# Tanh over runs of up to six W1 items, and the last output block's products and stores, in a fused attention and MLP kernel

## The chip, the cores and the metric

One core of one Trainium2 chip. The metric is the device time of one execution in microseconds (us). The engines are TensorE (PE, matrix products into the eight PSUM banks), VectorE (DVE), ScalarE (ACT), GpSimd (POOL) and SyncE (SP, which issues the transfers between HBM and the on-chip memory SBUF). Each engine works through its own instruction stream in order and waits on semaphores for the others.

## The reference

`x` is [1, 2048, 1024] in bf16, F is 3584, there are 32 heads of 32. The kernel computes

```
xn = layernorm(x)
s  = attention(xn; wqkv) @ wo            # softmax over 2048 keys, 32 heads
h  = gelu(layernorm(xn) @ w1 + b1)       # tanh form of gelu
g  = silu(h @ w2 + b2)
out = x + s * g
```

`layernorm` subtracts the mean and divides by the square root of variance + 1e-5, `gelu` is the approximation 0.5 x (1 + tanh(0.798 (x + 0.0447 x^3))).

## The kernel before, in words

**Two streams of work.** Attention runs over 8 groups of 4 heads, 8 blocks of 256 queries and 8 pairs of key blocks, 512 units in all. For each unit TensorE forms the scores of four heads (L902), ScalarE takes the exponential in two instructions over 128x1024 (L911), TensorE multiplies with V (L625), and VectorE adds the probabilities in a tree (L928, L942) from which TensorE forms the row sums. The last block of 256 queries is done in two halves of 128 (`half_unit`, L1197, with its scores at L1211 and exponentials at L1221), each closed by `half_quotient` (L1241): two 32x32 transposes, a reciprocal and a product on VectorE. Six PSUM banks hold scores, banks 6 and 7 take everything else in turn ("dense" work): projections, the MLP, P·V, the output projection.

**The MLP** runs beside attention in 8 chunks of 256 rows. A chunk has 14 W1 items (`w1_item`, L1074): sixteen matmuls of 128x128 by 256 columns into one bank (L630), then VectorE adds the bias and writes one of 20 slots of `hT` (L1084). Item p of the whole run uses slot p mod 20. Gelu follows on runs of neighbouring slots: five VectorE operations (L1098 square, L1099 times constant plus 1, L1100 times x, L1102 plus 1, L1103 times x) around one tanh on ScalarE (L1101) in one of two buffers `ut` of four items each. A run ends at every fourth slot, at a chunk's end, and at some fixed places, so it has four items (2048 elements a partition) or two (1024). The four W2 items of a chunk (`w2_item`, L1106) then read all its 14 slots, 56 matmuls each, and silu follows with one tanh per two items (L1128). `seq_mlp` (L1140) gives the order: six W1 items of the next chunk stand between the first three W2 items of this one and its fourth, eight behind that.

**What sets the order.** A planner written in Python (`_Plan`) simulates the five engines when the kernel is built, with a cost for every instruction, and emits each engine's stream as it comes out, with semaphore waits from declared reads and writes (tokens). ScalarE takes exponentials first (priority 0); a tanh that has been ready for 2500 ns of planned time goes ahead of them (L160). On TensorE scores go first, then P·V and dense items by position. So a change of one instruction can move all that follow. SP, too, gets one stream: weights, stores and loads stand in it in planned order, and a store that waits holds up those behind it.

**The end.** Output rows come in 16 blocks of 128; a block has two halves of 512 columns. Each half is eight products (one for each head group, `hc` 0 to 7) with the `wo` rows. For the last four blocks (`late`) the first seven go early into a bank as an item `most`, whose sum VectorE takes out to an f32 buffer `xf`, times 0.5 and the gate (L1439), and adds x (L1442). The eighth waits for the last attention quotient and goes alone into another bank; VectorE multiplies it by 0.5 and the gate (L1452) and adds `xf` (L1455). For the very last half (row block 15, second half, `i2 == 3`) ScalarE takes the eighth product out instead (L1447), and VectorE multiplies by the gate (L1449). The last two blocks, 14 and 15, are stored in four half stores `osl0` to `osl3` (L1458), each of 128x512. Each of them is declared to write the token list `rt` of its block's buffer, which the two halves of a block share; the second half's store therefore waits for the semaphore of the first half's.

Of the kernel before, what the change touches and what calls it, by code (L numbers as in the profile page):

```python
# [7 lines left out]
ALU = mybir.AluOpType  # L8
# [459 lines left out]
def bass_recurrent_scan__mha_block__mixer_channel_mlp__prompt_kernel(  # L468
# [31 lines left out]
    with ExitStack() as st:  # L500
# [60 lines left out]
        iota_i = ut_t[0][:].rearrange("p a b -> p (a b)")[:, 0:256].bitcast(I32)  # L561

        def bank(i, lo=0, hi=512):
            return ps[:, i * 512 + lo:i * 512 + hi]
# [498 lines left out]
        def make_y(c):  # L1063
            for t2 in range(2):
# [6 lines left out]
                dma(f"yt{t2}", lambda e, t2=t2: e.dma_start_transpose(yT[:, :, t2 * 128:(t2 + 1) * 128], yst_t[t2][:]),  # L1071
                    262144, [("yst", t2)], [("yT", t2)], occ=1300, rate=300.0, lat=2300)

        def w1_item(c, pi):  # L1074
            p = c * NW1 + pi
            gi, hs = p % NW1R, p % NH
            it = _Item("mlp")
            for f2 in range(2):
                for dc in range(DC):
                    def fn(e, b, f2=f2, dc=dc):  # L1080
                        return mm(e, bank(b, f2 * 256, (f2 + 1) * 256), w1r[:, gi, dc, f2 * 128:f2 * 128 + 128], yT[:, dc, :],
                                  dc == 0 and f2 == 0, dc == DC - 1)
# [7 lines left out]
            k = 2 if (pi == NW1 - 1 and p % 4 != 3) or (pi == 1 and c % 2) or half else 4  # L1090
            h0, n = hs - k + 1, k * 512
            hs_ = [("h", h0 + i) for i in range(k)]
            ui = geg["n"] % 2
            geg["n"] += 1
            x_ = hT[:, h0:h0 + k].rearrange("p s k t -> p (s k t)")
            u_ = ut_t[ui][:].rearrange("p a b -> p (a b)")[:, 0:n]
            gp, ga = (1.4, -1) if c == NCH - 1 and pi >= 5 else (3, 1)
            dve(lambda e: e.tensor_tensor(u_, x_, x_, op=ALU.mult), c_b16(n), hs_, [("ut", ui)], gp)  # L1098
            dve(lambda e: e.tensor_scalar(u_, u_, GA, 1.0, op0=ALU.mult, op1=ALU.add), c_b4(n), [("ut", ui)], [("ut", ui)], gp)  # L1099
            dve(lambda e: e.tensor_tensor(u_, u_, x_, op=ALU.mult), c_b16(n), [("ut", ui)] + hs_, [("ut", ui)], gp)  # L1100
            act(lambda e: e.activation(u_, u_, ACT.Tanh, scale=GC), c_acts(n), [("ut", ui)], [("ut", ui)], ga)  # L1101
            dve(lambda e: e.tensor_scalar_add(u_, u_, 1.0), c_b4(n), [("ut", ui)], [("ut", ui)], gp)  # L1102
            dve(lambda e: e.tensor_tensor(x_, u_, x_, op=ALU.mult), c_b16(n), [("ut", ui)] + hs_, hs_, gp)  # L1103
            return it

        def w2_item(c, q):  # L1106
# [211 lines left out]
        for w in range(HG):  # L1318
# [24 lines left out]
            for qb in range(NQB):  # L1343
# [44 lines left out]
                for t2 in range(2):  # L1388
# [16 lines left out]
                    for nh in range(2):  # L1405
                        late = qb >= NQB - 2
                        fin = qb == NQB - 1
                        it = _Item("wo", 64 * 7 + 8 * qb + 4 * t2 + 2 * nh)
                        i2 = 2 * t2 + nh
                        sl_ = slice(nh * 512, (nh + 1) * 512)  # L1410
                        if late:
                            most = _Item("wo", it.pos + 64)
                            plan.dense["last"].append(most)
                            if fin:
                                it.bank = 2 + 2 * t2 + nh
                                if not t2:
                                    it.due = 64 * HG - 2
                            (plan.dense["wo"] if not fin else lates if t2 else firsts).append(it)
                        for hc in range(HG):
                            def fn(e, b, hc=hc, tb=tb, nh=nh, late=late):  # L1420
# [3 lines left out]
                            chunk(most if late and hc < HG - 1 else it, fn, Q512,  # L1424
                                  [("OTr", hc) if hc < 7 else ("OTr", 7, qb) + ((t2,) if fin else ()), ("wo", hc)],
                                  [("S", 1 + t2, nh)] if fin and hc == HG - 1 else ())
                        if not late:
                            dve(lambda e, it=it, gr=gr, sl_=sl_: e.scalar_tensor_tensor(gr[:, sl_], bank(it.bank), 0.5,
                                                                                        gr[:, sl_], op0=ALU.mult, op1=ALU.mult),
                                c_ps(512), [], [("gr", ri, nh)], 0, it)  # L1430
                            dve(lambda e, xr=xr, gr=gr, sl_=sl_: e.tensor_tensor(xr[:, sl_], gr[:, sl_], xr[:, sl_], op=ALU.add),
                                c_b16(512), [("gr", ri, nh)], [("xr", ri, nh)], 1)
# [6 lines left out]
                        dve(lambda e, most=most, gr=gr, sl_=sl_, xf=xf: e.scalar_tensor_tensor(  # L1439
                            xf, bank(most.bank), 0.5, gr[:, sl_], op0=ALU.mult, op1=ALU.mult),  # L1440
                            c_ps(512), [("gr", ri, nh)], [("xf", xk)] + (zs if fin else []), 0, most)
                        dve(lambda e, xr=xr, sl_=sl_, xf=xf: e.tensor_tensor(xf, xf, xr[:, sl_], op=ALU.add),  # L1442
                            c_f32(512), [("xr", ri, nh)], [("xf", xk)], 2)
                        if fin and i2 == 3:
                            hs_ = fl3(PR[0])[:, i2 * 512:(i2 + 1) * 512]
                            after([("half", i2)], [("PR", 0)])
                            act(lambda e, it=it, hs_=hs_: e.activation(hs_, bank(it.bank), ACT.Copy, scale=0.5), c_act(512),  # L1447
                                [], [("half", i2)], 1, it)
                            dve(lambda e, gr=gr, sl_=sl_, hs_=hs_: e.tensor_tensor(gr[:, sl_], gr[:, sl_], hs_, op=ALU.mult),  # L1449
                                c_b16(512), [("half", i2)], [("gr", ri, nh)], -1 + 0.1 * i2)  # L1450
                        else:
                            dve(lambda e, it=it, gr=gr, sl_=sl_: e.scalar_tensor_tensor(gr[:, sl_], bank(it.bank), 0.5,  # L1452
                                                                                        gr[:, sl_], op0=ALU.mult, op1=ALU.mult),
                                c_ps(512), [], [("gr", ri, nh)], -1 if fin and t2 else 0, it)
                        dve(lambda e, xr=xr, gr=gr, sl_=sl_, xf=xf: e.tensor_tensor(xr[:, sl_], gr[:, sl_], xf, op=ALU.add),  # L1455
                            c_f32(512), [("gr", ri, nh), ("xf", xk)], [("xr", ri, nh)], -1 + 0.1 * i2 if fin and t2 else 2.05 if fin else 1)
                        if fin:
                          dma(f"osl{i2}", lambda e, xr=xr, tb=tb, sl_=sl_: e.dma_start(  # L1458
                            out2[tb * 128:(tb + 1) * 128, sl_], xr[:, sl_]), 131072, [("xr", ri, nh)], rt, prio=0, rate=390.0, lat=1000.0)
# [70 lines left out]
```

## Time and profile before

| | us |
|---|---|
| median of the runs shown | 1033.36 |
| lowest and highest of three | 1032.63, 1033.86 |
| the profiled execution | 1032.24 |
| its span, first to last instruction | 1030.3 |
| busy: TensorE, VectorE, ScalarE | 1004.7, 956.3, 1016.9 |
| mean granted TensorE clock | 0.997 |

The profile is one execution. Its page gives the busy time of each engine, the chain of work that ended last (followed back from the last instruction to what released each step), the costliest groups of instructions by line, and the transfers. A group's row reads: line, engine, operation, output tile <- input tiles, shapes, count | busy us, mean ns of one | idle us of the engine just before them, and what ended most of it. A tile's buffer number is left out. "PEld" is TensorE's weight load, which overlaps its products. Tanh instructions are the rows with `ut` (gelu) and `gw` (silu) on ScalarE.

### The profile page before, as it was taken

The numbers are of one execution on the slowest core, as the hardware profiler recorded it, in microseconds if no ns is written. First come the engines' busy times: TensorE is split into PE (matmuls) and PEld (weight loads), VectorE is DVE, ScalarE is ACT, GpSimd is POOL, SyncE is SP. The second block draws the span as 40 slices with busy tenths as digits, with TensorE's granted clock in tenths as the row PEclk, the third lists the DMA queues.
The fourth block names the chain that finished last, engine by engine and source line by source line (L and its number), as shares of the span: only waits on it lengthen the run. The fifth ranks groups of instructions, "written<-read, shape, count | busy, mean of one in ns | idle before, by whom it ended". The sixth has DMA issues, their size and how long they took to land.

```text
span 1030.3 us, 31971 instructions
## 1 busy us (share of the span) xinstructions
PE 1004.7 (98%) x14355; PEld 636.6 (62%) x14355; DVE 956.3 (93%) x1347; ACT 1016.9 (99%) x1093; POOL 11.8 (1%) x21
## 2 busy tenths in 40 slices
PE   8999999999999999999999999999999999999996
PEld 6666656666666567566665676666666665654443
DVE  8899999899899999997899989998999889978987
ACT  8999999999999999999999999999999999999996
POOL 2200000000000000000000000000000000000000
PEclk9999999999999999999999999999999999999999
DMA  8867746645765658456547576565455752974321
GB/s 222 158 156 206 200 136 182 170 117 142 204 175 154 182 157 228 125 144 188 139 126 195 143 215 173 158 177 152 118 154 167 216 168 78 279 224 124 112 91 58
DMA packets 317144, 167.75 MB, mean 163 GB/s; under 512 B 55632, under 2 KB 304976, under 8 KB 317008
## 3 DMA queue, kind: packets, MB, share of 16 engines
q1 hardware_dynamic: 317008, 165.71, 58.8%
q8 instruction: 112, 1.84, 0.7%
q14 instruction: 24, 0.20, 0.1%
HBM read 146.55 MB, written 12.06 MB: 154 GB/s over the span
## 4 chain that ended last, share of the span: by engine, by line
ACT 84%; PE 7%; DVE 5%; DMA 2%; issue 0%; SPq 0%; POOL 0%; DVEq 0%
ACT P L911 78%; PE ps L630 4%; ACT ut L1101 4%; PE ps L625 2%; ACT gw L1128 1%; PE ps L902 1%; ACT P L1221 1%; DVE PA L928 1%; DMA wv<-in_A_wqkv_dram 1%; DVE stats L837 1%; DVE PR L942 1%; DVE hT L1084 1%; DMA yst<-in_A_x_dram 1%; DVE gw L796 0%; DMA hT<-in_A_x_dram 0%; DMA xnT<-gw 0%
## 5 line engine op out<-in xcount | busy, mean ns | idle before, releaser
L911 ACT ACTIVATE P<-ps 128x1024 bf16<-128x1024 f32 x988 | 922.4, 1231 | 0.6 <-PE ps L902 0.5
L928 DVE TENSOR_TENSOR PA<-P 128x2048 bf16<-128x2048 bf16 x173 | 209.8, 1215 | 30.0 <-ACT P L911 29.5
L630 PE MATMUL ps<-yT,w1r 128*128 128x256 bf16 x1792 | 228.0, 273 | 0.9 <-DVE V L716 0.4
L630 PE MATMUL ps<-w2r,hT 128*128 128x256 bf16 x1792 | 224.3, 273 | 0.7 <-DVE nt L997 0.3
L942 DVE TENSOR_TENSOR PR<-PR,PA 128x2048 bf16<-128x2048 bf16 x173 | 209.1, 1210 | 1.2
L902 PE MATMUL ps<-QKT 32*128 32x256 bf16 x4032 | 200.4, 273 | 9.2 <-ACT P L911 7.0
L630 PEld LDWEIGHTS ps<-yT,w1r 128*128 128x128 bf16 x1792 | 164.5, 98 | 53.5 <-issue 28.1
L630 PEld LDWEIGHTS ps<-w2r,hT 128*128 128x128 bf16 x1792 | 163.0, 98 | 51.5 <-issue 31.3
L902 PEld LDWEIGHTS ps<-QKT 32*128 32x128 bf16 x4032 | 59.8, 92 | 137.3 <-ACT P L911 129.4
L625 PE MATMUL ps<-P,V 128*32 128x256 bf16 (+1 forms) x4080 | 137.2, 272 | 0.2
L630 PE MATMUL ps<-xnT,wqk 128*128 128x512 bf16 (+2 forms) x584 | 131.3, 354 | 1.1 <-DVE nv L1010 0.3
L625 PEld LDWEIGHTS ps<-P,V 128*32 128x32 bf16 x4080 | 95.6, 96 | 32.7 <-issue 22.6
L630 PE MATMUL ps<-wv,xnT 128*128 128x256 bf16 (+2 forms) x704 | 89.7, 267 | 1.6 <-DMA xnT<-gw 0.6
L630 PEld LDWEIGHTS ps<-xnT,wqk 128*128 128x128 bf16 x584 | 50.0, 98 | 50.7 <-issue 14.4
L1084 DVE TENSOR_TENSOR hT<-ps,b1T 128x512 bf16<-128x512 f32 x112 | 76.6, 684 | 3.7 <-PE ps L630 3.2
L928 DVE TENSOR_TENSOR PR<-P 128x2048 bf16<-128x2048 bf16 x60 | 72.7, 1212 | 0.1
L630 PEld LDWEIGHTS ps<-wv,xnT 128*128 128x128 bf16 x704 | 56.5, 99 | 25.6 <-issue 11.6
L1101 ACT ACTIVATE ut<-ut 128x2048 bf16<-128x2048 bf16 (+1 forms) x33 | 61.4, 1861 | 0.0
L728 DVE CAST QKT<-ps 128x512 bf16<-128x512 f32 x58 | 39.6, 683 | 1.6 <-PE ps L630 1.2
L997 DVE STREAM_TRANSPOSE nt<-ps 128x256 f32<-128x256 f32 x63 | 27.9, 442 | 13.8 <-PE ps L625 13.4
L1103 DVE TENSOR_TENSOR hT<-ut,hT 128x2048 bf16<-128x2048 bf16 (+1 forms) x33 | 34.6, 1049 | 0.1
L1098 DVE TENSOR_TENSOR ut<-hT 128x2048 bf16<-128x2048 bf16 (+1 forms) x33 | 34.7, 1050 | 0.1
(115 smaller groups left out, 584.9 us busy)
## 6 DMA issues: line engine op xcount, KB each, us to landing
w1r<-in_B_w_dram SPq DMA_DIRECT2D x112, 512.0 KB, 4.7
w2r<-in_B_w_dram SPq DMA_DIRECT2D x128, 448.0 KB, 4.5
yst<-in_A_x_dram SPq DMA_DIRECT2D x18, 256.0 KB, 4.7
wqk<-in_A_wqkv_dram SPq DMA_DIRECT2D x16, 256.0 KB, 3.7
g_scratch<-gw SPq DMA_DIRECT2D x32, 128.0 KB, 2.9
hT<-in_A_x_dram SPq DMA_DIRECT2D x14, 256.0 KB, 3.9
o_scratch<-ot SPq DMA_DIRECT2D x56, 64.0 KB, 3.6
xnT<-o_scratch SPq DMA_DIRECT2D x7, 512.0 KB, 5.3
```

The costliest lines, as they stand in the source:

```text
L625: ins = e.matmul(dst(j), lhsT=lhsT(j), rhs=rhs(j), start=start, stop=stop, tile_position=(0, 32 * j), skip_group_check=True)
L630: return e.matmul(dst, lhsT=lhsT, rhs=rhs, start=start, stop=stop, skip_group_check=True)
L728: dve(lambda e: e.tensor_copy(QKT[sl][:, which, tq * 512:(tq + 1) * 512], bank(it.bank)), c_ps(512), [], [(nm, sl, 2 * tq), (nm, sl, 2 * t ...
L902: ins = e.matmul(bank(b0[j], kk * 256, (kk + 1) * 256), lhsT=QKT[sl][32 * j:32 * j + 32, 1, kb * 128:(kb + 1) * 128], rhs=QKT[sl][32 * j:3 ...
L911: x = act(lambda e, h=h: e.activation(Pt[pi][:, 2 * h:2 * h + 2].rearrange("p j k q -> p (j k q)"), ps[:, pr[h] * 1024:(pr[h] + 1) * 1024] ...
L928: return dve(lambda e: e.tensor_tensor(dst[:].rearrange("p u j q -> p (u j) q"), src[:].rearrange("p u j k q -> p (u j) k q")[:, :, 0, :], ...
L942: return dve(lambda e: e.tensor_tensor(fl3(pr), fl3(pr), fl3(PA[i]), op=ALU.add), c_b16(2048), [("PA", i), tok], [tok], 3.2)
L997: dve(lambda e: e.transpose(nt_t[:], bank(pv.bank, 256, 512)), c_ps(256) + 120, [], [("nt",)], prio, pv)
L1084: w1_ev[p] = dve(lambda e: e.tensor_tensor(hT[:, hs], bank(it.bank).rearrange("p (k t) -> p k t", k=2), b1T[:, 2 * pi:2 * pi + 2].unsqueez ...
L1098: dve(lambda e: e.tensor_tensor(u_, x_, x_, op=ALU.mult), c_b16(n), hs_, [("ut", ui)], gp)
L1101: act(lambda e: e.activation(u_, u_, ACT.Tanh, scale=GC), c_acts(n), [("ut", ui)], [("ut", ui)], ga)
L1103: dve(lambda e: e.tensor_tensor(x_, u_, x_, op=ALU.mult), c_b16(n), [("ut", ui)] + hs_, hs_, gp)
```

## The change

Three edits.

1. A table `GRUNS` is made ahead, which says at which item a gelu run ends and how many items it has: up to six in chunks 0 to 5, up to four in chunks 6 and 7, never across the end of the ring of 20 slots, and in the last chunk two at a time where four or fewer are left. The two buffers `ut` become the halves of one tile of eight items. A run over four is cut into a part of four and a part of two for VectorE's five operations; the tanh is one instruction over the whole run (3072 elements a partition for six items).
2. In the last output block's second half (`whole`), the eight products go into one bank: the seven early ones are no longer taken out, so that half has no L1439 and no L1442. `it`, the item of the eighth product, takes over the bank of `most`; ScalarE's copy, the gate's product and a single bf16 add of x finish it.
3. The half stores write no shared token any more; each waits only for its own data.

```diff
+        GMAX = 6
-        ut_t = [sb(f"ut{i}", [128, 4, 512], BF16) for i in range(2)]
+        utw = sb("ut", [128, 8, 512], BF16)
+        ut_t = [utw[:, 4 * i:4 * i + 4] for i in range(2)]
...
+        GRUNS = {}
+        for c_ in range(NCH):
+            p_, end = c_ * NW1, (c_ + 1) * NW1
+            while p_ < end:
+                k_ = min(GMAX if c_ < 6 else 4, end - p_, NH - p_ % NH)
+                if c_ == NCH - 1:
+                    k_ = min(k_, 2 if end - p_ <= 4 else 4)
+                GRUNS[p_ + k_ - 1] = k_
+                p_ += k_
...
-            half = c == NCH - 1 and pi in (NW1 - 3, NW1 - 1)
-            if p % 4 != 3 and pi != NW1 - 1 and not (pi == 1 and c % 2) and not half:
+            run = GRUNS.get(p)
+            if run is None:
                 return it
...
+            for h0 in range(hh, hh + run, 4):
+                k = min(4, hh + run - h0)
+                ui = 0 if h0 > hh or run > 4 else geg["n"] % 2
+                parts.append([h0, k, ui])
+            if run > 4:
+                parts[1][2] = 1
+                geg["n"] = 0
+            else:
+                geg["n"] += 1
...
+            ua = utw[:, u0:u0 + run].rearrange("p a b -> p (a b)")
+            act(lambda e: e.activation(ua, ua, ACT.Tanh, scale=GC), c_acts(run * 512), uts, uts, ga)
...
+                        whole = fin and i2 == 3
                         if late:
-                            most = _Item("wo", it.pos + 64)
-                            plan.dense["last"].append(most)
-                            if fin:
+                            most = _Item("wo", it.pos + (100 if whole else 64))
+                            if not whole:
+                                plan.dense["last"].append(most)
+                            if whole:
+                                most.heirs, most.evacs = (it,), it.evacs
+                                plan.dense["pre"] = [most]
+                            elif fin:
                                 it.bank = 2 + 2 * t2 + nh
...
-                                          wo_at[hc][:, nh * 512:(nh + 1) * 512], hc == 0 or late and hc == HG - 1,
-                                          hc == HG - 1 or late and hc == HG - 2)
+                                          wo_at[hc][:, nh * 512:(nh + 1) * 512], hc == 0 or late and not whole and hc == HG - 1,
+                                          hc == HG - 1 or late and not whole and hc == HG - 2)
...
+                        if whole:
+                            dve(lambda e, xr=xr, gr=gr, sl_=sl_: e.tensor_tensor(xr[:, sl_], gr[:, sl_], xr[:, sl_], op=ALU.add),
+                                c_b16(512), [("gr", ri, nh)], [("xr", ri, nh)], -1 + 0.1 * i2)
+                        else:
+                            dve(lambda e, xr=xr, gr=gr, sl_=sl_, xf=xf: e.tensor_tensor(xr[:, sl_], gr[:, sl_], xf, op=ALU.add),
+                                c_f32(512), [("gr", ri, nh), ("xf", xk)], [("xr", ri, nh)], -1 + 0.1 * i2 if fin and t2 else 2.05 if fin else 1)
                         if fin:
                           dma(f"osl{i2}", lambda e, xr=xr, tb=tb, sl_=sl_: e.dma_start(
-                            out2[tb * 128:(tb + 1) * 128, sl_], xr[:, sl_]), 131072, [("xr", ri, nh)], rt, prio=0, rate=390.0, lat=1000.0)
+                            out2[tb * 128:(tb + 1) * 128, sl_], xr[:, sl_]), 131072, [("xr", ri, nh)], [], prio=0, rate=390.0, lat=1000.0)
```

More of the change, by code (lines that the diff above doesn't have):

```diff
@@ L1096, in w1_item @@
-            u_ = ut_t[ui][:].rearrange("p a b -> p (a b)")[:, 0:n]
-            gp, ga = (1.4, -1) if c == NCH - 1 and pi >= 5 else (3, 1)
[L1098 to L1101, printed above, removed]
@@ new lines, in w1_item @@
+            if run > 4:
[3 more added lines that the diff above has]
+                geg["n"] += 1
+            views = []
+            for h0, k, ui in parts:
+                hs_ = [("h", h0 + i) for i in range(k)]
+                n = k * 512
+                x_ = hT[:, h0:h0 + k].rearrange("p s k t -> p (s k t)")
+                u_ = utw[:, 4 * ui:4 * ui + k].rearrange("p a b -> p (a b)")
+                views.append((x_, u_, n, hs_, ui))
+                dve(lambda e, u_=u_, x_=x_: e.tensor_tensor(u_, x_, x_, op=ALU.mult), c_b16(n), hs_, [("ut", ui)], gp)
+                dve(lambda e, u_=u_: e.tensor_scalar(u_, u_, GA, 1.0, op0=ALU.mult, op1=ALU.add), c_b4(n), [("ut", ui)], [("ut", ui)], gp)
+                dve(lambda e, u_=u_, x_=x_: e.tensor_tensor(u_, u_, x_, op=ALU.mult), c_b16(n), [("ut", ui)] + hs_, [("ut", ui)], gp)
@@ new lines, in w1_item @@
+            u0 = 4 * parts[0][2]
+            ua = utw[:, u0:u0 + run].rearrange("p a b -> p (a b)")
+            uts = [("ut", q_[2]) for q_ in parts]
+            act(lambda e: e.activation(ua, ua, ACT.Tanh, scale=GC), c_acts(run * 512), uts, uts, ga)
+            for x_, u_, n, hs_, ui in views:
+                dve(lambda e, u_=u_: e.tensor_scalar_add(u_, u_, 1.0), c_b4(n), [("ut", ui)], [("ut", ui)], gp)
+                dve(lambda e, u_=u_, x_=x_: e.tensor_tensor(x_, u_, x_, op=ALU.mult), c_b16(n), [("ut", ui)] + hs_, hs_, gp)
@@ L1419, in bass_recurrent_scan__mha_block__mixer_channel_mlp__prompt_kernel, with fn @@
                         for hc in range(HG):
-                            def fn(e, b, hc=hc, tb=tb, nh=nh, late=late):
+                            def fn(e, b, hc=hc, tb=tb, nh=nh, late=late, whole=whole):
                                 return mm(e, bank(b), OTr[:, hc, tb * 128:tb * 128 + 128],
-                                          wo_at[hc][:, nh * 512:(nh + 1) * 512], hc == 0 or late and hc == HG - 1,
-                                          hc == HG - 1 or late and hc == HG - 2)
+                                          wo_at[hc][:, nh * 512:(nh + 1) * 512], hc == 0 or late and not whole and hc == HG - 1,
+                                          hc == HG - 1 or late and not whole and hc == HG - 2)
                             chunk(most if late and hc < HG - 1 else it, fn, Q512,
                                   [("OTr", hc) if hc < 7 else ("OTr", 7, qb) + ((t2,) if fin else ()), ("wo", hc)],
-                                  [("S", 1 + t2, nh)] if fin and hc == HG - 1 else ())
+                                  [("S", 1 + t2, nh)] if fin and hc == HG - 1 and not whole else ())
                         if not late:
@@ L1438, in bass_recurrent_scan__mha_block__mixer_channel_mlp__prompt_kernel @@
                             after([("xf", xk)], [("w1", i) for i in range(NW1R)])
[L1439 to L1443, printed above, removed]
+                        if not whole:
+                            dve(lambda e, most=most, gr=gr, sl_=sl_, xf=xf: e.scalar_tensor_tensor(
+                                xf, bank(most.bank), 0.5, gr[:, sl_], op0=ALU.mult, op1=ALU.mult),
+                                c_ps(512), [("gr", ri, nh)], [("xf", xk)] + (zs if fin else []), 0, most)
+                            dve(lambda e, xr=xr, sl_=sl_, xf=xf: e.tensor_tensor(xf, xf, xr[:, sl_], op=ALU.add),
+                                c_f32(512), [("xr", ri, nh)], [("xf", xk)], 2)
                         if fin and i2 == 3:
```

14 lines of the change are left out of this document (3 added, 11 removed).

## The prediction

> **What bounds the kernel now.** I read the page's head first, then the chain of work that ended last by engine, then ScalarE's instructions grouped by shape, then busy time in stretches.
>
> ```profile
> span 1030.3 us, 31971 instructions
> PE 1004.7 (98%) x14355; PEld 636.6 (62%) x14355; DVE 956.3 (93%) x1347; ACT 1016.9 (99%) x1093; POOL 11.8 (1%) x21
> ACT 84%; PE 7%; DVE 5%; DMA 2%; issue 0%; SPq 0%; POOL 0%; DVEq 0%
> ```
>
> Three engines are nearly full, so the busy shares alone do not decide; the chain does: 84% of it is ScalarE (ACT).
>
> ```profile
> L911 ACT ACTIVATE P<-ps 128x1024 bf16<-128x1024 f32 x988 | 922.4, 1231 | 0.6 <-PE ps L902 0.5
> L1101 ACT ACTIVATE ut<-ut 128x2048 bf16<-128x2048 bf16 x23 | 48.6, 2113 | 0.0
> L1101 ACT ACTIVATE ut<-ut 128x1024 bf16<-128x1024 bf16 x10 | 12.8, 1281 | 0.0
> ```
>
> 988 exponentials were preceded by 0.6 us of idle in all, and no tanh by any. In the middle of the run ScalarE has no gap at all (columns: stretch, its length, then busy us and count of PE, weight loads, DVE, ACT, POOL; granted clock, DMA share, GB/s):
>
> ```profile
> 400.00:440.00 40.00, 39.49 (x519) 25.03 (x518) 38.04 (x51) 40.00 (x44) 0.00 (x0) 1.00 0.59 159
> 520.00:560.00 40.00, 39.70 (x564) 24.63 (x553) 39.91 (x57) 40.00 (x43) 0.00 (x0) 1.00 0.63 162
> 840.00:880.00 40.00, 38.68 (x497) 22.54 (x497) 39.69 (x60) 40.00 (x43) 0.00 (x0) 1.00 0.36 106
> ```
>
> In the last of these the chain runs over TensorE and VectorE, yet ScalarE still issued 43 instructions there, as many as between 520 and 560: the three engines are balanced, and ScalarE is not held up. So time leaves the body only if ScalarE gets less work, and comes back if anything makes it wait. What one of its instructions costs is the step from one start to the next, read from the pieces of the chain (start, length, what):
>
> ```profile
> 567.38 0.94 ACT ut L1101
> 568.31 16.50 ACT P L911 x18
> 619.68 1.79 ACT ut L1101
> 925.70 81.58 ACT P L911 x89
> ```
>
> An exponential takes a slot of 81.58/89 = 0.917 us, a tanh over 2048 elements 1.79, one over 1024 elements 0.94. The mean durations (1231, 2113, 1281 ns) are longer, because consecutive instructions overlap.
>
> ScalarE's idle time, 1030.3 - 1016.9 = 13.4 us, lies at the two ends: 40 - 34.83 = 5.2 us in the first stretch, 30.3 - 22.54 = 7.8 us in the last.
>
> ```profile
> 0.00:40.00 40.00, 35.17 (x479) 27.13 (x483) 33.31 (x87) 34.83 (x45) 9.79 (x20) 0.96 0.81 196
> 1000.00:1040.00 40.00, 21.93 (x546) 11.50 (x543) 23.62 (x45) 22.54 (x25) 0.00 (x0) 0.95 0.12 41
> ```
>
> After the last exponential comes the tail: a chain over TensorE, VectorE and the queue of stores, up to 1030.3. The timeline gives the last eleven exponentials (start, length), which end at 1011.58 + 10.37 = 1021.95:
>
> ```profile
> 1011.58 10.37 ACT L1221 ACTIVATE P<-ps 128x1024 bf16<-128x1024 f32 x11
> ```
>
> **Part one: tanh on up to six items.** Before, 33 tanh: 23 x 4 + 10 x 2 = 112 items of 512 elements. After, by the runs that the new table forms, 27: ten of six items, nine of four, eight of two, again 112 items. The elements are the same, so what goes is the fixed part of six instructions. From the two slots, 1024 more elements cost 1.79 - 0.94 = 0.85 us, so the fixed part is 0.94 - 0.85 = 0.09 us: 6 x 0.09 = **0.5 us** less on the bounding engine. No row has a 3072-element tanh; by the slots it takes 1.79 + 0.85 = 2.64 us. The bounds of the fixed part: nothing at the low end, and at the high end the mean durations taken at face value, 1281 - (2113 - 1281) = 449 ns, 2.7 us for six. I take the slots, because only starts count on an engine that never idles.
>
> The Trainium skill's page "ScalarE: Activation LUTs" (Rules for kernel authors) budgets about 0.3 us per ACTIVATE besides 0.83 ns an element; by that six of them would save some 1.8 us, an estimate from that page, and the sum below would be 2.7 instead of 1.4. The same page (What ACT_TABLE_LOAD costs) lets neighbours overlap by about 93 ns of 186, which is what the slots here agree with.
>
> VectorE keeps working on at most four items at a time, so a run of six is a group of four and one of two: 33 groups become 19 of four and 18 of two, five operations each.
>
> ```profile
> L1098 DVE TENSOR_TENSOR ut<-hT 128x2048 bf16<-128x2048 bf16 x23 | 27.9, 1212 | 0.1
> L1099 DVE TENSOR_SCALAR ut<-ut 128x2048 bf16<-128x2048 bf16 x23 | 15.6, 676 | 0.0
> L1098 DVE TENSOR_TENSOR ut<-hT 128x1024 bf16<-128x1024 bf16 x10 | 6.8, 677 | 0.0
> L1099 DVE TENSOR_SCALAR ut<-ut 128x1024 bf16<-128x1024 bf16 x10 | 4.0, 404 | 0.0
> ```
>
> Four groups of four become eight of two: 8 x 677 - 4 x 1212 = 568 ns for each of three tensor-tensor operations and 8 x 404 - 4 x 676 = 528 ns for each of two scalar ones, 2.8 us more on VectorE at most. Its cover is its own idle time, 1030.3 - 956.3 = 74 us; in a stretch where it is at 39.9 of 40 us this can be late, and what is late next is the evacuation of a W1 bank, then TensorE, then ScalarE's next scores. I cost it at nothing. Giving both gelu buffers one tile, and the index pattern a place in it, adds no instruction. TensorE gets none either. Its first 1060 matmuls and its last 3258 stand in the same order in both programs, as do ScalarE's first 93 instructions (to about 88 us) and its last 162; between these the planner has laid everything out anew, loads of weights among it. A tanh of six items waits for six evacuations instead of four, and the W2 products that need them come up to two items later; they are covered as long as TensorE has projections, scores or P·V to do. That is the risk, priced under the rivals.
>
> **Parts two and three: the tail.** The last rows of before:
>
> ```profile
> 1014.50 1.88 DVE L1455 TENSOR_TENSOR hT<-hT,w1r 128x512 bf16<-128x512 bf16 x3
> 1020.23 0.69 DVE L1439 SCALAR_TENSOR_TENSOR gw<-ps,hT 128x512 f32<-128x512 f32 x1 [0.60 <-PE ps L630]
> 1020.26 0.59 PE L630 MATMUL ps<-yst,xnT 128*128 128x512 bf16 x2
> 1020.84 1.28 DVE L1452 SCALAR_TENSOR_TENSOR hT<-ps,hT 128x512 bf16<-128x512 f32 x2
> 1022.03 0.68 DVE L1442 TENSOR_TENSOR gw<-gw,hT 128x512 f32<-128x512 f32 x1
> 1022.80 0.32 DVE L1245 STREAM_TRANSPOSE nt<-ps 128x128 f32<-128x128 f32 x1
> 1024.06 0.60 PE L630 MATMUL ps<-yst,xnT 128*128 128x512 bf16 x2 [1.31 <-DVE xnT L1255]
> 1024.52 0.68 DVE L1452 SCALAR_TENSOR_TENSOR hT<-ps,hT 128x512 bf16<-128x512 f32 x1
> 1024.70 0.60 ACT L1447 ACTIVATE PR<-ps 128x512 bf16<-128x512 f32 x1 [2.75 <-PE ps L630]
> 1025.23 0.69 DVE L1455 TENSOR_TENSOR hT<-hT,gw 128x512 bf16<-128x512 bf16 x1
> 1025.84 0.42 DVE L1449 TENSOR_TENSOR hT<-hT,PR 128x512 bf16<-128x512 bf16 x1
> 1026.29 1.29 DVE L1455 TENSOR_TENSOR hT<-hT,gw 128x512 bf16<-128x512 bf16 x2
> 1024.62 0.33 SPq L1458 DMA_DIRECT2D out_dram<-hT  x1
> 1025.95 0.33 SPq L1458 DMA_DIRECT2D out_dram<-hT  x1
> 1027.61 0.33 SPq L1458 DMA_DIRECT2D out_dram<-hT  x1
> 1027.99 0.43 SPq L1458 DMA_DIRECT2D out_dram<-hT  x1
> ```
>
> The third store waits for the very last add, the second half of row block 14 (1026.29 + 1.29 = 1027.58), and the fourth, the last half of block 15, stands behind it in the queue although its add ended 0.6 us earlier. In the changed order the evacuation L1439 and its add L1442 are gone, and both adds of block 14 stand where these two stood. That is four VectorE operations before the last quotient as before, but they now start with the product of the pair at 1020.26, not with the evacuation at 1020.23. The pair at 1024.06 lets VectorE start 0.46 later, so the first begins at 1020.72; four slots of (1.88 - 0.68)/2 = 0.60 end at 1023.12. The transpose began at 1022.80, when TensorE's last sums were there: **0.32 later**. Between 0 (the start could have been earlier, VectorE was busy at 1024.52) and 0.5 (a drain after each dependent pair), I keep 0.32.
>
> From there all steps move by 0.32 up to the multiply L1449, now at 1026.16. The last add follows 0.45 later, at 1026.61, and is bf16 on both inputs, like this row:
>
> ```profile
> L1431 DVE TENSOR_TENSOR QKT<-QKT 128x512 bf16<-128x512 bf16 x16 | 6.4, 417 | 0.1
> ```
>
> So it ends at 1027.03 and its store goes out at 1027.06. The other three stores are out by then: block 14's from about 1022.6 on, and the third at 1025.95 + 0.32 = 1026.27, 0.8 before. The last store of before went out at 1027.99: **0.93 us gained**; what follows it (1030.3 - 1027.99 = 2.3 us, landing and end) stays. Bounds: 0.75 with 0.5 of delay, 1.25 with none.
>
> **The sum**: 0.5 + 0.93 = 1.4 us. The profiled execution took 1032.24 us around its span of 1030.3; it would become 1030.8, with a span of 1028.9. It lies 1.1 us under the median of the three runs shown, so against the median, 1033.36, I forecast **1031.9 us**. 0.2% of it, about what a measurement of this kernel can tell from no change, is 2.1 us.
>
> **Rivals.** (B) *More than the slots say.* The fixed part of a tanh may be larger than 0.09 us in effect: each is also a block in which no bank of scores is emptied, and six fewer leave TensorE and VectorE calmer where the chain is on them now (12% of it). Since ScalarE's idle time lies at the two ends, fractions of a microsecond are to be had in the body beside fewer slots. Between 0.5 and 2.7 us for the six, 1.5 as the middle: 2.4 in all, **1030.9**. Against it speaks that the slots are exact: 16.50/18 is 0.917 too. The 1.8 us that follow from the Trainium skill's figure above lie inside this rival's bounds.
>
> (C) *The larger groups starve TensorE: slower.* Place: the six chunks with runs of six. The ring holds 20 items, a chunk has 14; the last items of a chunk can only be written when W2 of the chunk before has read its own, and that waits for the tanh of a whole run.
>
> ```profile
> 845.50 3.27 PE ps L630 x29
> ```
>
> One matmul takes 0.113 us, an item of sixteen 1.8. If TensorE runs dry for one item in half of the ten runs of six, five stalls cost 9 us; since TensorE is idle only 0.3 to 1.3 us in the 40 us stretches above, a stall beyond about 1 us is not made up and reaches ScalarE. Half of it filled by projections: 4.5 - 1.4 = 3.1 slower, **1036.5**. For it: VectorE at 39.9 of 40 us in the gelu stretches. Against it: the same matmuls, the same end from ScalarE's last 162 instructions on, and shorter last runs (two or four items) at each chunk's end, just ahead of the W2 products.
>
> (D) *The tail gives nothing*: VectorE's four operations delay the last quotient by the full 0.9. Then only 0.5 is left, **1032.9**.
>
> **How the numbers follow.** Forecast 0.55, B 0.27, C 0.13, D 0.05. The forecast's own range is 1031.2 to 1032.6 (tail bounds, and the scatter of 0.6 us either way that the three runs show). For 8 in 10 it reaches down to B less a little scatter, 1030.5, and up to D with some, 1033.3; C's time is left out. Faster by over 0.2% (below 1031.3) is most of B and some of the forecast's scatter, 0.33; slower by over 0.2% is C and a little, 0.14; the rest, 0.53, lies within.
>
> **What would show it.** Right: 27 tanh on ScalarE, those over 3072 elements stepping 2.64 us on the chain; ScalarE 40.00 of 40 in every stretch from 80 to 1000 us; the last exponential ending 0.5 us earlier; the last quotient's transpose 0.3 later after it than now; the last store going out 5.1 us after the end of the last exponential instead of 6.0. Wrong: idle time ahead of exponentials released by TensorE or VectorE between 88 and 880 us (C), a 3072-element tanh well off 2.64 (B), or the last two stores within 0.4 us of each other (D).

## The result

The changed kernel takes 1031.04 us (median of 15 runs, 1028.9 to 1032.72), the kernel before, measured beside it, 1033.21 (1032.11 to 1035.31): ratio 0.9976, 95% interval 0.9968 to 0.9983, so 2.5 us less, between 1.8 and 3.3 (the two medians alone differ by 2.2). The forecast was 1031.9, 1.4 us less. Timed twice more, against other runs of before, the changed kernel gave 0.9967 (0.9955 to 0.9979) and 0.9982 (0.9973 to 0.9992).

The head of the page after:

```profile
span 1029.6 us, 31985 instructions
PE 1004.2 (98%) x14355; PEld 635.9 (62%) x14355; DVE 956.8 (93%) x1365; ACT 1016.6 (99%) x1087; POOL 11.8 (1%) x21
ACT 78%; PE 10%; DVE 7%; DMA 4%; issue 1%; POOL 0%; SPq 0%
```

ScalarE still bounds, with six instructions fewer. VectorE has 18 more (20 for gelu, two less in the tail) and is 0.5 us busier; the 2.8 us of the prediction were an upper bound. Loads (DMA) now hold 4% of the chain.

ScalarE by shape, after (count, busy us, mean ns, idle before):

```profile
L913 ACT ACTIVATE P<-ps 128x1024 bf16<-128x1024 f32 x988 | 921.3, 1228 | 0.8 <-PE ps L904 0.7
L1127 ACT ACTIVATE ut<-ut 128x3072 bf16<-128x3072 bf16 x10 | 30.1, 3012 | 0.0
L1127 ACT ACTIVATE ut<-ut 128x2048 bf16<-128x2048 bf16 x9 | 19.3, 2146 | 0.0
L1127 ACT ACTIVATE ut<-ut 128x1024 bf16<-128x1024 bf16 x8 | 10.1, 1267 | 0.0
```

There are 27 tanh, none of them waited for. On the chain of waits after they take as much as forecast, 2.64 us for six items:

```profile
431.88 2.64 ACT ut L1127
434.52 14.67 ACT P L913 x16
449.19 0.93 ACT ut L1127
...
512.50 1.79 ACT ut L1127
```

The tail after, from the timeline (start, length; in the first row the last sixteen exponentials, which end at 1007.46 + 14.90 = 1022.36; the last row is the last store, from SyncE's timeline):

```profile
1007.46 14.90 ACT L1248 ACTIVATE P<-ps 128x1024 bf16<-128x1024 f32 x16
...
1020.67 0.59 PE L632 MATMUL ps<-yst,xnT 128*128 128x512 bf16 x2
1021.09 1.29 DVE L1485 SCALAR_TENSOR_TENSOR hT<-ps,hT 128x512 bf16<-128x512 f32 x2 [1.03 <-PE ps L632]
1022.29 1.28 DVE L1492 TENSOR_TENSOR hT<-hT,gw 128x512 bf16<-128x512 bf16 x2
1023.50 0.31 DVE L1272 STREAM_TRANSPOSE nt<-ps 128x128 f32<-128x128 f32 x1
1024.75 0.60 PE L632 MATMUL ps<-yst,xnT 128*128 128x512 bf16 x2 [1.58 <-DVE xnT L1282]
1025.17 0.69 DVE L1485 SCALAR_TENSOR_TENSOR hT<-ps,hT 128x512 bf16<-128x512 f32 x1 [0.48 <-PE ps L632]
1025.90 0.69 DVE L1492 TENSOR_TENSOR hT<-hT,gw 128x512 bf16<-128x512 bf16 x1
1026.51 0.42 DVE L1482 TENSOR_TENSOR hT<-hT,PR 128x512 bf16<-128x512 bf16 x1
1026.96 0.42 DVE L1489 TENSOR_TENSOR hT<-hT 128x512 bf16<-128x512 bf16 x1
1027.41 0.33 SPq L1495 DMA_DIRECT2D out_dram<-hT  x1
```

Count from the end of the last exponential, because the body in front shifts from one execution to the next. The last quotient's transpose starts 1023.50 - 1022.36 = 1.14 us after it; before, it was 1022.80 - 1021.95 = 0.85. The last store goes out 5.05 after it instead of 6.04, and the span ends 7.26 after it instead of 8.35.

**The two parts of the span in each profile.** "Body" is from the start of the first exponential to the end of the last, "tail" from there to the end of the span, all in us:

| kernel | body, first to last | body | last store | tail |
|---|---|---|---|---|
| before | 13.21 to 1021.95 | 1008.7 | +6.04 | 8.4 |
| changed | 13.46 to 1022.36 | 1008.9 | +5.05 | 7.3 |
| changed, second | 12.97 to 1021.01 | 1008.0 | +5.05 | 7.3 |
| changed, third | 13.27 to 1022.11 | 1008.8 | +5.05 | 7.3 |
| tanh runs alone | 13.34 to 1023.38 | 1010.0 | +6.05 | 8.4 |
| tail edits alone | 13.48 to 1022.14 | 1008.7 | +5.05 | 7.4 |
| stores alone | 13.60 to 1023.12 | 1009.5 | +5.67 | 7.8 |
| one bank alone | 13.62 to 1025.06 | 1011.4 | +6.04 | 8.2 |
| changed, tanh split | 13.02 to 1021.31 | 1008.3 | +5.05 | 7.3 |
| changed, add moved | 13.47 to 1021.39 | 1007.9 | +4.94 | 7.1 |
| changed, add moved, again | 13.30 to 1023.50 | 1010.2 | +4.94 | 7.2 |
| changed, add moved, reloads later | 13.35 to 1023.66 | 1010.3 | +6.06 | 8.2 |
| before, normalisations later | 13.53 to 1022.96 | 1009.4 | +6.11 | 8.4 |
| before, tanh in pieces | 13.58 to 1028.01 | 1014.4 | +6.46 | 8.8 |

The tail is 8.4 us where neither tail edit is in (8.8 with the tanh in pieces) and 7.1 to 7.4 where both are. The one exception with both, the reloads later, has another order at its end (experiment 9). The body scatters by 2 to 3 us: the kernel with the moved add, profiled twice, shows 1007.9 and 1010.2. That is more than the 0.5 us that the tanh are worth. That is why the pair of profiles in this section, taken alone, shows 0.8 us (1032.24 and 1031.42) and no gain in the body.

### The profile page after: what moved, and what is told of

Read it like the earlier page. It is cut to its first block, busy times and chain, and to the rows that moved or that the text cites. A ratio compares the mean times of both kernels' runs of the same rounds, so it can differ in the third digit from the quotient of the medians.

```text
span 1029.6 us, 31985 instructions
## 1 busy us (share of the span) xinstructions
PE 1004.2 (98%) x14355; PEld 635.9 (62%) x14355; DVE 956.8 (93%) x1365; ACT 1016.6 (99%) x1087; POOL 11.8 (1%) x21
## 4 chain that ended last, share of the span: by engine, by line
ACT 78%; PE 10%; DVE 7%; DMA 4%; issue 1%; POOL 0%; SPq 0%
ACT P L913 71%; PE ps L632 7%; ACT ut L1127 4%; DMA w2r<-in_B_w_dram 3%; PE ps L904 2%; DVE stats L839 1%; PE ps L627 1%; ACT P L1248 1%; DVE PA L930 1%; ACT gw L1155 1%; DVE PR L944 1%; DMA xnT<-gw 1%; DVE gw L798 1%; ACT w2r L913 1%; DMA hT<-in_A_x_dram 0%
## 5 line engine op out<-in xcount | busy, mean ns | idle before, releaser
L1127 ACT ACTIVATE ut<-ut 128x3072 bf16<-128x3072 bf16 (+2 forms) x27 | 59.6, 2206 | 0.0
```

Source lines behind the costliest of these rows:

```text
L1127: act(lambda e: e.activation(ua, ua, ACT.Tanh, scale=GC), c_acts(run * 512), uts, uts, ga)
```

## The experiments

**1. The tanh runs alone** (`e1_tanh_only`): the first edit on the kernel before; the streams of TensorE, ScalarE and SyncE are those of the changed kernel.

> The kernel before with the first edit alone (tanh on runs of up to six items); the tail is that of before, and TensorE, ScalarE and SyncE have the order of the changed kernel. Theory 1, the slots: six tanh fewer at 0.09 us give 0.5 us less, ratio 0.9995, and the rest of the measured 2.2 us is the tail and scatter. Theory 2, the new order of the body does more than the slots say: 1.2 us less or more, ratio 0.9988 or lower. Rival, larger groups starve TensorE: slower than before. In the profile theory 1 expects the time from the first exponential to the end of the last one 0.5 us shorter than the 1008.7 of before.

Measured: ratio 0.9998 (0.9989 to 1.0006). Theory 1's 0.9995 lies inside, theory 2's 0.9988 just outside; a slowdown by starved TensorE is not seen beyond 0.6 us. No change at all lies inside too, so this timing does not show the 0.5 us by itself. The body of its profile did not shrink by 0.5 but is 1.3 us longer than before's, which the table shows to be within the scatter.

**2. The tail edits alone** (`e2_tail_only`): the second and third edit on the kernel before.

> The kernel before with the second and third edit alone (last half in one bank, stores without the shared token); the tanh runs and the orders of TensorE, ScalarE and SyncE are those of before. Theory 1: the tail alone gives 1.0 to 1.1 us, ratio 0.9990; last store issued 5.1 us after the end of the last exponential (6.0 before), span ending 7.2 after it (8.35 before). Theory 2 expects the same 1.0 here. If instead the tail is what exceeded the forecast: 1.7 us or more less.

Measured: ratio 0.9995 (0.9987 to 1.0004), tail 7.4 against 8.4, last store at +5.05, as in the changed kernel; its issue took 0.52 us instead of 0.33, which is why this tail is 0.2 longer than that of the changed kernel. Theory 1's 0.9990 lies inside the interval, no change does too, and 1.7 us less is outside. What shows the gain is the tail of the profile, not this timing.

**3. The changed kernel with the tanh split again** (`e4_after_split`): same planned order, other emission.

```diff
-            act(lambda e: e.activation(ua, ua, ACT.Tanh, scale=GC), c_acts(run * 512), uts, uts, ga)
+            def th(e):
+                for a_, b_ in ((0, min(run, 4) * 512), (2048, run * 512)):
+                    if a_ < b_:
+                        ins = e.activation(ua[:, a_:b_], ua[:, a_:b_], ACT.Tanh, scale=GC)
+                return ins
+            act(th, c_acts(run * 512), uts, uts, ga)
```

> The changed kernel with each of the ten six-item tanh issued as one over four items and one over two: 37 tanh instead of 27, every engine in the planned order of the changed kernel. Theory 1, only the fixed part of the instructions counts: 10 x 0.09 = 0.9 us slower than the changed kernel, so 0.7 us less than before, ratio 0.9993. Theory 2, the new order helps by itself: it keeps most of the gain, 1.5 us less than before or better, ratio 0.9986 or lower.

Measured: 0.9992 (0.9982 to 1.0002), theory 1's 0.9993. It does not exclude theory 2's 0.9986, which lies inside too, nor no change.

**4. Before with every tanh in pieces of one item** (`e5_before_pieces`): the price of the fixed part made large enough to be measured, in the planned order of before.

```diff
-            act(lambda e: e.activation(u_, u_, ACT.Tanh, scale=GC), c_acts(n), [("ut", ui)], [("ut", ui)], ga)
+            def th(e):
+                for a_ in range(0, n, 512):
+                    ins = e.activation(u_[:, a_:a_ + 512], u_[:, a_:a_ + 512], ACT.Tanh, scale=GC)
+                return ins
+            act(th, c_acts(n), [("ut", ui)], [("ut", ui)], ga)
```

> The kernel before with every gelu tanh issued in pieces of one item, 112 instead of 33, in the planned order of before: it measures the fixed part of a tanh. Slots of the chain, 0.09 us each: 79 x 0.09 = 7.1 us slower, ratio 1.0069. Fixed part hidden by something else: no change. Fixed part as the mean durations say, 0.45 us: 35 us slower.

Measured: 1.0066 (1.0053 to 1.0079), 6.8 us for 79 instructions, **0.086 us each** (0.069 to 0.103). Its group of tanh and one run of four pieces on its chain:

```profile
L1103 ACT ACTIVATE ut<-ut 128x512 bf16<-128x512 bf16 x112 | 68.2, 834 | 0.0
```

```profile
87.30 2.03 ACT ut L1103 x4
```

Four pieces hold the chain for 2.03 us where one instruction over the same four items took 1.79: 0.08 us for each of the three that came on top. From start to start the trace gives the same without the chain's rounding: 0.520 us for one item here, 0.947, 1.800 and 2.653 for two, four and six items in the kernels before and after, which is 0.094 us and 0.4265 for each item. The mean duration of a piece, 834 ns, would have said 4 x 834 - 2113 = 1.2 us. The slot is the price, the duration is not.

**5. The stores alone** (`e3_stores_only`), one profiled execution: `rt` in the list of what the half stores write becomes `[]`, the rest is before.

> The kernel before with the third edit alone: half stores without the shared token. Theory: the third store in SyncE's queue still waits for the very last add of VectorE, and the fourth stands behind it, so the last store goes out 6.0 us after the end of the last exponential and the span ends 8.35 after it, both as before. Rival, the waits of stores for each other are what the tail costs: last store 0.4 to 1.0 us earlier.

The last add and the last store of its timeline:

```profile
1027.47 1.29 DVE L1455 TENSOR_TENSOR hT<-hT,gw 128x512 bf16<-128x512 bf16 x2
```

```profile
1028.79 0.33 SPq L1458 DMA_DIRECT2D out_dram<-hT  x1
```

The last store goes out at +5.67 instead of 6.04, the tail is 7.8: the theory missed by 0.4 us, and the rival holds at its lower end. Without the token the four stores stand in the queue as their adds end, so the store of the last half leaves before the last add (1027.47 + 1.29 = 1028.76), and only one store follows it. Before, two left after it, 0.38 apart (1027.61 and 1027.99).

**6. One bank alone** (`e6_bank_only`), one profiled execution: the second edit on before, the token kept.

> The kernel before with the second edit alone: the last half's eight products in one bank, half stores still with the shared token. Theory: the adds end as early as in the changed kernel (last one 5.0 us after the last exponential), but the last store waits for the semaphore of the third, which goes out 4.3 us after the last exponential and takes 1.7 to land: last store at about 6.1, no gain over 6.0. Rival, the shorter chain on VectorE alone makes the gain: last store at 5.1 as in the changed kernel.

```profile
1029.66 0.42 DVE L1462 TENSOR_TENSOR hT<-hT 128x512 bf16<-128x512 bf16 x1
```

```profile
1031.10 0.33 SPq L1468 DMA_DIRECT2D out_dram<-hT  x1
```

How long the four half stores of this kernel took from issue to landing:

```profile
DMA to landing us min/median/max: 1.7/1.7/3.1
```

The last add ends at 1030.08, the last store leaves 1.0 us later, at +6.04. The half store before it had left 1.8 us earlier, at +4.25, so the last one left just when that had landed: its own data was ready, it waited for the other half. In the same way the second half of block 14 left 3.1 us after the first, the one store that took 3.1 to land. So the second edit gains nothing without the third, the third 0.4 us without the second, both together 1.0.

**7. The add of block 14's second half moved behind the last quotient** (`e8_add_moved`), on the changed kernel.

```diff
-                                c_f32(512), [("gr", ri, nh), ("xf", xk)], [("xr", ri, nh)], -1 + 0.1 * i2 if fin and t2 else 2.05 if fin else 1)
+                                c_f32(512), [("gr", ri, nh), ("xf", xk)] + ([("OTr", w, qb, 1)] if fin and i2 == 1 else []), [("xr", ri, nh)],
+                                -1 + 0.1 * i2 if fin and t2 else 2.05 if fin else 1)
```

> The changed kernel with one edit: the add of row block 14's second half waits for the last attention quotient, so VectorE does it while TensorE forms the last two products. Theory: the last quotient's first transpose starts with TensorE's last sums again, about 0.3 us earlier against the last exponential than in the changed kernel (1.14 us after its end there, 0.8 expected), the add itself hides behind the products, and the last store goes out 4.75 us after the last exponential instead of 5.06. Rival: VectorE only shifts the 0.6 us of the add behind the quotient, and the last store stays at 5.0 or later.

```profile
1022.24 0.32 DVE L1272 STREAM_TRANSPOSE nt<-ps 128x128 f32<-128x128 f32 x1 [0.24 <-PE ps L627]
...
1023.48 0.69 DVE L1492 TENSOR_TENSOR hT<-hT,gw 128x512 bf16<-128x512 bf16 x1
1024.09 0.68 DVE L1485 SCALAR_TENSOR_TENSOR hT<-ps,hT 128x512 bf16<-128x512 f32 x1
```

The transpose starts 0.86 after the last exponential (1021.38) again, and even waits for TensorE: the 0.3 us are the price of VectorE's fourth operation. But the add does not hide wholly: it waits for the quotient to be written (1023.15 + 0.29), starts 0.04 after that and keeps VectorE until 1024.09, while TensorE's pair had started at 1023.50. Of the 0.3 only 0.1 stays; last store at +4.94, tail 7.1. The rival's 5.0 or later did not come either. Timed (`e11_add_moved_again`):

> The changed kernel with the add of row block 14's second half behind the last quotient, as looked at once before, now timed: 0.1 us less than the changed kernel by its tail (4.95 against 5.06 us from the last exponential to the last store), which is below what the comparison can tell; ratio to before 0.9978.

Measured: 0.9985 (0.9975 to 0.9996), beside 0.9982 of the changed kernel against the same runs of before. As expected, 0.1 us cannot be told.

**8. The changed kernel twice more** (`e7_after_again`, `e12_after_third`).

> The changed kernel once more against before. Theory 1, slots and tail make the change and the rest of the first 2.2 us was scatter: 1.4 to 1.6 us less, ratio 0.9985. Theory 2, the order of the body brings more: 2.2 us less again, ratio 0.9978 or lower.

> The changed kernel a third time, beside the two others of this call. Slots 0.5, tail 1.1 and the load's wait at 83 us 0.6 (theory 3): 2.2 us less than before, ratio 0.9979. Slots and tail alone: 1.6 us, ratio 0.9985. As the second time: 3.3 us, ratio 0.9967.

Measured: 0.9967 (0.9955 to 0.9979) and 0.9982 (0.9973 to 0.9992). The first speaks for more than slots and tail (1.6 us, 0.9985), the second is compatible with them.

**9. Three reloads later** (`e9_loads_later`): the changed kernel with the moved add, and three of the six reloads of the attention output behind the W2 loads.

```diff
-                [("o_d", hc, q) for q in range(NQB)], [("OTr", hc)], extra=dead, rate=390.0, lat=3700.0)
+                [("o_d", hc, q) for q in range(NQB)], [("OTr", hc)], extra=dead + ([w2_loads[122]] if 3 <= hc < 6 else []),
+                rate=390.0, lat=3700.0)
```

> The changed kernel with the moved add of the run before and one more edit: three of the six reloads of the attention output that are issued together at 876 us wait until the W2 loads before the last eight are in. Theory: the W2 waits on TensorE between 880 and 920 us (0.6 to 1.2 us beyond the slots on ScalarE in four profiles) shrink to about 0.2, and the tail gains 0.3: about 0.8 us less than the changed kernel. Rival: the reloads come late for the output projection, and ScalarE waits between 905 and 940 us instead.

Measured: 1.0002 (0.9990 to 1.0015), where the changed kernel against the same runs of before had 0.9967: 3.6 us slower than that. What TensorE and ScalarE waited for between 880 and 925 us (total, times, longest), in this kernel:

```profile
PE ps L632 <- DMA w2r<-in_B_w_dram: 2.4, 1, 2.4
...
ACT P L913 <- PE ps L904: 2.2, 3, 1.1
```

and in the changed one:

```profile
PE ps L632 <- DMA w2r<-in_B_w_dram: 0.9, 2, 0.6
```

```profile
906.35 9.29 DMA w2r<-in_B_w_dram
```

The last line is a piece of the chain of waits in the experiment's profile: the moved reloads came between the last W2 loads, and one of these holds 9.29 us of the chain. The wait grew instead of shrinking, and ScalarE waited where the rival had said, between 905 and 925 us. The plan behind it changed as well, and the tail lost its gain (8.2). The attempt failed on both counts.

**10. The wait at 83 us** (`e10_norm_later`). Three profiles with the order of before show ScalarE short between 80 and 120 us, and VectorE waiting for a load at 83 us. In the tail-edits-alone kernel, which has the body of before, VectorE's, TensorE's and ScalarE's waits of that stretch were:

```profile
DVE yst L1068 <- DMA yst<-in_A_x_dram: 1.5, 2, 1.3
```

```profile
PE ps L902 <- DVE hT L1084: 1.4, 1, 1.4
```

```profile
ACT P L911 <- PE ps L902: 0.9, 1, 0.9
```

One stall goes through three engines: the normalisation stands ahead of the bias add that empties a bank of W1, the next matmuls on TensorE stand behind that bank, and the scores behind those. The experiment takes the two normalisations six instructions later in VectorE's stream:

```diff
+        vq = plan.order["DVE"]
+        at = vq.index(yn[3])
+        anchor = vq[at + 6]
+        for seq_ in (vq, plan.seq):
+            for o in yn[2:4]:
+                seq_.remove(o)
+            k = seq_.index(anchor) + 1
+            seq_[k:k] = yn[2:4]
         plan.settle()
```

> The kernel before with one thing moved in VectorE's stream: the two normalisations of the second chunk's rows (tile yst) stand six instructions later, after the PR add, as about where the changed order has them. All other streams are those of before. Theory 3: in the order of before they wait at 83 us for their load (0.2 to 1.3 us in the profiles), and the W1 evacuation, TensorE and ScalarE's scores behind them wait too; moved, no wait on that load is left, ScalarE loses nothing beyond its slots between 80 and 120 us (0 to 1.3 us, 0.6 on average, in five profiles with the order of before; 0 in six with the changed one), and the kernel is 0.6 us faster than before, ratio 0.9994. Rival: the loss only moves to the next late instruction, ScalarE still loses about 0.6 us there or just behind, ratio 1.0000.

Measured: 1.0001 (0.9992 to 1.0009). The stretch from 80 to 120 us (busy us and count of PE, weight loads, DVE, ACT, POOL; clock, DMA share, GB/s) in the tail-edits-alone kernel, this one, and the changed one:

```profile
80.00:120.00 40.00, 37.89 (x552) 25.36 (x554) 38.51 (x52) 39.03 (x41) 0.00 (x0) 1.00 0.67 184
```

```profile
80.00:120.00 40.00, 38.61 (x555) 26.06 (x555) 39.33 (x54) 39.81 (x42) 0.00 (x0) 1.00 0.70 192
```

```profile
80.00:120.00 40.00, 39.87 (x573) 26.61 (x572) 39.75 (x58) 40.00 (x43) 0.00 (x0) 1.00 0.74 200
```

The load's wait is gone, and ScalarE still has idle time; what TensorE waits for now is VectorE itself:

```profile
PE ps L630 <- DVE V L716: 0.6, 1, 0.6
PE ps L625 <- DVE QKT L728: 0.5, 1, 0.5
```

Summing each step between starts less its slot (0.917, 0.94 and 1.79 us, as in the prediction), ScalarE loses 0.5 us there, as in two other profiles with the order of before (0.6 and 0.6). Theory 3 falls as a cause, the rival holds: the load's wait was one of several late instructions in a stretch where VectorE is full. All three profiles of the changed kernel lose nothing there (under 0.05).

## Why the prediction was right

**The tanh.** Count and step are as forecast (27; 2.64 us), and the fixed part, 0.09 us, is confirmed by experiment 4 at 0.086: 0.5 us for six. Rival B's larger figures for it, up to 0.45 us, are excluded. The Trainium skill's page "ScalarE: Activation LUTs", in the section "What ACT_TABLE_LOAD costs", gives 186 ns for an ACTIVATE with immediate scale and bias, less about 93 ns for one behind another; the 93 ns that are left, an estimate from that page, agree with the 0.086 us. Its budget of 0.3 us, in "Rules for kernel authors", lies outside the measured interval; the page gives it for a bias passed as a pointer operand, a condition that the prediction leaves out, and these tanh are passed no bias.

**The tail.** The last quotient came 0.3 later (forecast 0.32), the last store went out at 5.05 (forecast 5.1). The gain in the last store's issue is 0.99 us, by the span's end 1.1; the term of 0.93 was 0.2 too small. The last store of before took 0.43 us to issue and that of after 0.33, and that much also came off its end. Rival D is out: the last two stores are 0.8 us apart. Experiments 5 and 6 bear out that both edits are needed, and correct one detail: the stores alone were worth 0.4 in the one profile taken.

**The body.** That ScalarE stays full was nearly right. The statement that it would be 40.00 us busy in every stretch from 80 to 1000 us failed in two, by 0.1 to 0.2 us: 680 to 720 (39.88) and 880 to 920 (39.83), where W2 loads came late. The first of them is, strictly, the sign named for rival C, an exponential that waited 0.12 us for TensorE, but behind a late load and not behind a tanh. The last exponential was to end 0.5 us earlier; in the profile it ended 0.4 later, in the two others at 1021.01 and 1022.11 against 1021.95, so a single profile could not show this. Rival C did not come: tanh wait for nothing, and the tanh runs alone are not slower beyond 0.6 us.

One premise was weaker than it looked: a ScalarE that is busy 40.00 of 40 us can still lose time. An exponential lasts 1.23 us but the next one can start after 0.904, so a hold-up of up to about 0.3 us does not show as idle time. The 0.917 of the prediction is an average over steps of 0.904, 0.920 and some near 1.04. Between 120 and 880 us the steps exceed the shortest ones by 9.1 us in all before and by 9.5 after. What lengthens them stays open; the change did not remove it.

**The sum.** Tail 1.1 and tanh 0.5 make 1.6 us. The three comparisons say 2.5 (1.8 to 3.3), 3.4 (2.2 to 4.7) and 1.9 (0.8 to 2.8). The two priced mechanisms are borne out; the total is not explained by them. The median, 1031.04, lies below the forecast's own range (1031.2 to 1032.6), inside the range for 8 in 10 that left room for rival B, and next to B's 1030.9, although B's larger fixed part is excluded and the calmer body that it also offered is not seen in the profiles. That the total fell inside the wider range is in part luck.

The term that could hold the rest is the body's: the new order was costed at nothing. The profiles put something on it in one place, between 80 and 120 us, where the order of before loses 0 to 1.3 us of ScalarE in six profiles (0.5 on average, experiment 10 among them) and the changed one nothing in three. But over the whole body nothing is left of it. Six profiles with the changed order and 27 tanh (changed, three times; tanh runs alone; add moved, twice) have a body of 1009.0 us on average, five with the order of before and 33 tanh (before, tail edits alone, stores alone, one bank alone, normalisations later) 1009.5. The difference, 0.6 us, is what the six tanh are worth; with bodies that scatter by 2 to 3 us, such averages cannot exclude a microsecond more. Experiment 1, which has that order, gained 0.2 us (-0.6 to 1.1), and experiment 10 did not find one instruction responsible. The parts and the whole were also not timed on the same chip: on that of experiments 1 to 4 the parts add up to 0.7 us (0.2 and 0.5), and the second and third comparison of the whole change come from two other chips; for the first, no chip is recorded. Where the 0.3 to 1.8 us above the sum come from stays open.

## What to carry to other kernels

On an engine that never idles, price an instruction by the step from its start to the next start, not by its duration: an added tanh cost 0.086 us, where the durations said 0.4. Nor did a busy share of 100% mean here that nothing was lost: hold-ups shorter than the overlap of two instructions do not show in it. In the last microseconds look at the queue of stores as at an engine: a shorter chain of arithmetic was worth nothing while the last store waited for the one before it, and the two edits together were worth 1.0 us. Where a profile pair differs by less than the scatter of the body, split the span at the last instruction of the bounding engine and compare the parts.

## What was not expected of the hardware

The body of one and the same order differs by 2 to 3 us from one execution to the next, and most of it lies in two places, the first 80 us (1.3 to 4.3 us beyond the shortest steps, in fourteen profiles) and 880 to 920 us (0.8 to 1.8, and 3.0 in experiment 9). Both are where loads are dense: the DMA engines are busy for 0.8 to 0.9 of the time there, and for 0.35 to 0.75 elsewhere up to 1000 us. In the second, SyncE's stream itself stood still: in the changed kernel's profile the 64 KB store issued at 882 us held the queue for 5 us.

```profile
880.77 1.54 SPq L1061 DMA_DIRECT2D w2r<-in_B_w_dram  x2
882.35 5.12 SPq L1287 DMA_DIRECT2D o_scratch<-ot  x1
887.52 0.66 SPq L1061 DMA_DIRECT2D w2r<-in_B_w_dram  x1
```

Of the 474 issues in this profile 362 take 0.44 us or less and 43 over 1 us; no other exceeds 3. This one takes 4.4 to 5.6 us in every profile but one. Six reloads of 512 KB, and three other loads, had been issued within the 6 us before it. The exception is experiment 9, where three of the six reloads come later: there the same store takes 0.95 us, and the slow issues (2.2 to 2.4 us) come at 906 to 911 us, behind the moved reloads. So an issue can be held up by transfers that are already under way, and the loads behind it in the queue leave late by as much.
